# A fused scan-and-mixture kernel: identity products ahead of the first pair, the first pair's gates in halves, and another hand-set order of the first three pairs

## The chip, the cores and the metric

The kernel runs on one core of one Trainium2 chip. The metric is the device time of one execution in microseconds; the runs of the kernel before took 177.32, 178.34 and 179.44 us (median 178.34). The engines are called as in the profile: PE is TensorE, ACT is ScalarE, DVE is VectorE, POOL is GpSimd, SP issues the transfers.

## The reference, cut to what matters

Four sequences with eight heads of 768 positions and 48 channels go through a gated linear recurrence, and its output, as 3072 rows of 384 channels, through a soft mixture of 8 experts.

```python
f = 1.0 / (1.0 + np.exp(-f_logit))
for t in range(S):
    state = f[:, :, t, :, None] * state + np.einsum('bhd,bhe->bhde', k[:, :, t], v[:, :, t])
    y[:, :, t] = np.einsum('bhd,bhde->bhe', q[:, :, t], state)
...
logits = x @ phi
d = softmax of logits over the rows;  slot_input = d.T @ x
slot_out[e] = np.maximum(slot_input[e] @ w1[e], 0.0) @ w2[e]
c = softmax of logits over the slots; return c @ slot_out
```

## The kernel before, in words

The 32 heads are handled as 16 pairs, two heads side by side in the partitions (112 rows used), 768 positions along the free dimension in six chunks of 128. A pair has these steps, each with a short name in the planner:

- loads of f, k, q and v (`lf`, `lk`, `lq`, `lv`), each one transfer on SP's queue.
- The gates. `e` and `ln` (lines 312, 315, ACT): exp and logarithm, with the sum of the exp kept as a guard. `L` (line 319, DVE): the running sum of the logarithms inside each chunk, restarted by a tile `starts` of ones and zeros. `g` and `p` (lines 322, 325, ACT): its exp with both signs, into `gb` and `pb`. `dk` and `dq` (lines 329, 333, POOL): k and q times those. `pbx` and `pend` (lines 342, 339, POOL): the chunk-end values of `pb`, spread for the state scan, and kept as a guard.
- The products. `kt` (line 347, PE): six transposes of k, copied to `kta` by `kte` (line 305, DVE). `sc` (line 359, PE) in two halves of three chunks: the scores, masked by `mask` (line 364, DVE). `kv` (line 393, PE): each chunk's contribution to the state; `scan` (line 397, DVE) runs the state over the chunks. `ia` (line 384, PE) and `ie` (line 407, PE): y from the masked scores and from the state of the chunk before. `ye` (line 305, ACT) copies y out.
- For the mixture: `lg` (line 439) the logits, `xtr` and `xe` (lines 418, 305) the transposed rows. After each four pairs a batch's softmax and slot sums follow. The expert products (`up`, `down`) and the output come behind the last pair.

The pairs overlap: while PE is in pair i, the gates of pairs i+1 to i+3 are under way. Buffers rotate (three of `fb`, `kb`, `qb`; two of `Lb`, `gb`, `pb`, `pbx`). PE's results go to five units of PSUM, which a product takes and the last reader frees.

The order of each engine's queue is set by a planner, run when the program is built: every step of the pairs has one engine and a due time (`z = 7 i` us plus an offset), and on each engine the fixed steps are emitted in order of due time. Weight loads and the end are placed by the planner's estimates of durations, as are the moments to which weight loads are held back. So a changed due time moves a step in its engine's queue, and all engines work their queues in order.

Of the kernel before, what the change touches and what calls it, by code (L numbers as in the profile page):

```python
# [10 lines left out]
AF = mybir.ActivationFunctionType  # L11
ALU = mybir.AluOpType
# [4 lines left out]
NM = S // C  # L17
# [6 lines left out]
PW = 112  # L24
# [178 lines left out]
NW1 = 7  # L203


@with_exitstack
def gla_soft_moe_kernel(ctx: ExitStack, tc: tile.TileContext, q, k, f, v, vt, phi, w1, w2, out):
# [28 lines left out]
    esum = P([PW, NP], "esum")  # L236
# [66 lines left out]

    def copy(o, dst, src):
        {"ACT": nc.scalar.copy, "DVE": nc.vector.tensor_copy, "POOL": nc.gpsimd.tensor_copy}[o.eng](dst, src)  # L305
# [5 lines left out]
    def decay_exp(o, i):  # L311
        nc.scalar.activation(fb[i % N_F][:PW], fb[i % N_F][:PW], AF.Exp, scale=-1.0, accum_out=esum[:, i : i + 1])  # L312

    def decay_ln(o, i):
        nc.scalar.activation(fb[i % N_F][:PW], fb[i % N_F][:PW], AF.Ln, bias=one[:PW])  # L315

    def decay_sum(o, i):

        nc.vector.tensor_tensor_scan(Lb[i % N_L][:PW], flat(starts)[:PW], fb[i % N_F][:PW], 0.0, op0=ALU.mult, op1=ALU.add)  # L319

    def decay_g(o, i):
        nc.scalar.activation(gb[i % N_G][:PW], Lb[i % N_L][:PW], AF.Exp)  # L322

    def decay_p(o, i):
        nc.scalar.activation(pb[i % N_P][:PW], Lb[i % N_L][:PW], AF.Exp, scale=-1.0)  # L325

    def decay_k(o, i):
        t = kb[i % N_K][:PW]
        nc.gpsimd.tensor_tensor(t, t, gb[i % N_G][:PW], op=ALU.mult)  # L329

    def decay_q(o, i):
        t = qb[i % N_Q][:PW]
        nc.gpsimd.tensor_tensor(t, t, pb[i % N_P][:PW], op=ALU.mult)  # L333
# [7 lines left out]
    def decay_pbx(o, i):  # L341
        nc.gpsimd.tensor_copy(pbx[i % N_S][:PW, :, : NM - 1], ends(i)[:, : NM - 1].unsqueeze(1).broadcast_to([PW, D, NM - 1]))

    def kt(o, i):
        u = unit(("kt", i))
        for m in range(NM):
            nc.tensor.transpose(u[:, C * m : C * m + PW], kb[i % N_K][:PW, C * m : C * m + C], ident[:PW, :PW])  # L347
# [353 lines left out]

    op("consts", {"DVE": 0.5}, lambda o: consts(), w=["same"], due=30)
    op("consts_2", {"POOL": 1.0}, lambda o: consts_2(), w=["emask"], due=40)

    def attention(i):

        z = i * T
        F_, L_, G, PB = ("fb", i % N_F), ("Lb", i % N_L), ("gb", i % N_G), ("pb", i % N_P)
        K, Q, V, Y = ("kb", i % N_K), ("qb", i % N_Q), ("vb", i % N_V), ("yT", i % N_Y)
# [47 lines left out]
    def mixture(b, z):  # L757
# [97 lines left out]
    PENDS = [(n, i) for i in range(NP) for n in ("pends", "esum")]  # L855
# [38 lines left out]
    order = plan.run(dict(POOL=2.0, DVE=1.0, ACT=1.3))  # L894
# [20 lines left out]
    by_pair = [[o for o in order if first_op[i] <= o.n < first_op[i] + 28 and o.name in ("ye", "lg", "xtr", "xe")] for i in range(NP)]  # L915
# [115 lines left out]
```

## Time and profile before

| what | value |
|---|---|
| runs | 177.32, 178.34, 179.44 us |
| profiled execution | 179.07 us, span 177.3 us |
| PE busy | 153.5 us, 87% |
| DVE busy | 111.8 us, 63% |
| ACT busy | 94.6 us, 53% |
| POOL busy | 94.0 us, 53% |
| from HBM, to HBM | 48.87 MB, 4.72 MB, 302 GB/s over the span |
| pair 0, first transpose to pair 1's first | 11.52 to 21.04 us |
| steady pair | 6.30 us |

The page has one line for each engine with its busy share in forty slices of 4.43 us. The chain of work that ended last is followed back from the end: each row has its start, its length, and the engine, tile and line. The timeline has start, length, engine, line, operation and output<-inputs, and in brackets how long the engine was idle before and what ended that. The table of windows has, for each stretch, its length, the busy time of an engine with its count of instructions, the granted clock of PE as a share (PEclk), the share of the transfer engines and GB/s. The granted clock is read as 1.00 before its first record in this execution, so the start's clock is read from the durations of PE's instructions instead.

### The profile page before, as it was taken

What the parts mean: (1) busy time and instruction counts of PE and PEld (TensorE: products, weight loads), DVE (VectorE), ACT (ScalarE), POOL (GpSimd) and SP (SyncE); (2) the same over time, 40 slices, a digit from 0 to 9 for tenths busy, and PEclk for the clock granted to TensorE, in tenths of its full rate; (3) what the DMA queues carried; (4) which work ended last, traced back from release to release, by engine and by line L of the source; (5) the groups of instructions that cost most, each with busy time, mean ns of one, the idle gap of its engine ahead of it and who ended that gap; (6) DMA issues with size and microseconds to landing.
All of it is one profiled execution on the core that took longest, in us unless ns stands there. A gap on an engine that the chain in (4) does not pass through costs nothing.

```text
span 177.3 us, 6018 instructions
## 1 busy us (share of the span) xinstructions
PE 153.5 (87%) x2538; PEld 123.0 (69%) x2538; DVE 111.8 (63%) x161; ACT 94.6 (53%) x164; POOL 94.0 (53%) x91
## 2 busy tenths in 40 slices
PE   0039999999899999999999999999899999987830
PEld 0029899889689887898896988787645448555720
DVE  2569697797996795989986977956320420552320
ACT  3995279668579576794976784132521210261510
POOL 3099999998759959786898895801000000100000
PEclk9999999999999999999999999999999999999875
DMA  5999999999999999999986569999993870058580
GB/s 180 352 409 358 332 330 322 408 398 401 387 403 384 384 379 398 374 398 398 325 274 189 180 203 352 385 354 380 398 401 133 269 263 4 4 229 311 214 324 12
DMA packets 20324, 54.08 MB, mean 305 GB/s; under 512 B 2256, under 2 KB 2368, under 8 KB 20288
## 3 DMA queue, kind: packets, MB, share of 16 engines
q1 hardware_dynamic: 20288, 53.60, 82.2%
q8 instruction: 22, 0.36, 0.8%
q14 instruction: 14, 0.11, 0.2%
HBM read 48.87 MB, written 4.72 MB: 302 GB/s over the span
## 4 chain that ended last, share of the span: by engine, by line
PE 77%; DVE 6%; issue 4%; POOL 4%; ACT 4%; DMA 2%; POOLq 0%; DVEq 0%; ACTq 0%
PE sc L359 13%; PE y L384 13%; PE y L407 7%; PE kv L393 6%; PE po L644 6%; PE up L600 6%; PE kt L347 5%; PE pf L688 5%; PE xt L418 4%; PE pl L439 3%; POOL ce L525 2%; DMA fb<-in_f_dram 2%; PE pi L482 2%; DVE same L294 1%; PE turn L617 1%
## 5 line engine op out<-in xcount | busy, mean ns | idle before, releaser
L329 POOL TENSOR_TENSOR kb<-kb,gb 112x768 f32<-112x768 f32 x16 | 41.3, 2582 | 13.7 <-ACT gb L322 12.8
L319 DVE TENSOR_TENSOR_SCAN Lb<-starts,fb 112x768 f32<-112x768 f32 x16 | 30.0, 1873 | 6.2 <-ACT fb L315 6.1
L333 POOL TENSOR_TENSOR qb<-qb,pb 112x768 f32<-112x768 f32 x16 | 30.1, 1881 | 4.5 <-ACT pb L325 4.5
L364 DVE TENSOR_TENSOR scb<-sc,mask 128x768 f32<-128x768 f32 x32 | 29.1, 951 | 4.1 <-PE sc L359 4.0
L359 PE MATMUL sc<-qb,kb 48*128 48x128 f32 x384 | 27.6, 291 | 1.6 <-DVE kta L305 1.2
L384 PE MATMUL y<-scb,va 128*64 128x128 f32 (+1 forms) x384 | 27.1, 285 | 0.4 <-DVE scb L364 0.4
L305 ACT COPY yT<-y 112x768 f32<-112x768 f32 x16 | 12.8, 800 | 27.3 <-PE y L407 27.3
L525 POOL TENSOR_TENSOR ce<-ce,cm 128x256 f32<-128x256 f32 x4 | 5.1, 1272 | 41.8 <-DVE cm L522 41.2
L359 PEld LDWEIGHTS sc<-qb,kb 48*128 48x128 f32 x384 | 24.0, 196 | 4.4 <-DVE kta L305 1.5
L384 PEld LDWEIGHTS y<-scb,va 128*64 128x64 f32 (+1 forms) x384 | 23.3, 135 | 1.0 <-issue 0.5
L347 PE MATMUL kt<-ident,kb 112*128 112x112 f32 x96 | 13.0, 274 | 11.5 <-POOL kb L329 11.5
L305 DVE COPY kta<-kt 128x672 f32<-128x672 f32 x16 | 13.7, 854 | 13.3 <-PE kt L347 13.3
L347 PEld LDWEIGHTS kt<-ident,kb 112*128 112x128 f32 x96 | 10.1, 145 | 12.5 <-POOL kb L329 11.5
L315 ACT ACTIVATE fb<-fb,one 112x768 f32<-112x768 f32 x16 | 15.0, 937 | 0.6
L393 PE MATMUL kv<-va,kta 128*64 128x48 f32 (+1 forms) x384 | 15.0, 225 | 0.0
L312 ACT ACTIVATE fb<-fb 112x768 f32<-112x768 f32 x16 | 13.4, 840 | 2.8 <-DMA fb<-in_f_dram 2.8
L407 PE MATMUL y<-qb,sb 48*48 48x128 f32 x320 | 14.6, 285 | 0.0
L393 PEld LDWEIGHTS kv<-va,kta 128*64 128x64 f32 (+1 forms) x384 | 13.0, 135 | 2.0 <-issue 0.2
L325 ACT ACTIVATE pb<-Lb 112x768 f32<-112x768 f32 x16 | 13.5, 845 | 0.0
L322 ACT ACTIVATE gb<-Lb 112x768 f32<-112x768 f32 x16 | 13.2, 828 | 0.0
L407 PEld LDWEIGHTS y<-qb,sb 48*48 48x48 f32 x320 | 11.1, 162 | 2.9 <-DVE sb L397 2.2
L305 ACT COPY xb<-xt 128x576 f32<-128x576 f32 x16 | 10.2, 639 | 5.0 <-PE xt L418 5.0
(145 smaller groups left out, 253.9 us busy)
## 6 DMA issues: line engine op xcount, KB each, us to landing
w1b<-in_w_dram SPq DMA_DIRECT2D x34, 384.0 KB, 6.8
fb<-in_f_dram SPq DMA_DIRECT2D x16, 384.0 KB, 6.2
kb<-in_k_dram SPq DMA_DIRECT2D x16, 384.0 KB, 6.5
qb<-in_q_dram SPq DMA_DIRECT2D x16, 384.0 KB, 6.5
va<-in_v_dram SPq DMA_DIRECT2D x16, 288.0 KB, 6.7
out_dram<-w1b SPq DMA_DIRECT2D x12, 384.0 KB, 3.0
scb<-in_w_dram SPq DMA_DIRECT2D x4, 384.0 KB, 5.8
fb<-in_w_dram SPq DMA_DIRECT2D x3, 384.0 KB, 3.8
```

Source lines behind the costliest of these rows:

```text
L305: {"ACT": nc.scalar.copy, "DVE": nc.vector.tensor_copy, "POOL": nc.gpsimd.tensor_copy}[o.eng](dst, src)
L315: nc.scalar.activation(fb[i % N_F][:PW], fb[i % N_F][:PW], AF.Ln, bias=one[:PW])
L319: nc.vector.tensor_tensor_scan(Lb[i % N_L][:PW], flat(starts)[:PW], fb[i % N_F][:PW], 0.0, op0=ALU.mult, op1=ALU.add)
L325: nc.scalar.activation(pb[i % N_P][:PW], Lb[i % N_L][:PW], AF.Exp, scale=-1.0)
L329: nc.gpsimd.tensor_tensor(t, t, gb[i % N_G][:PW], op=ALU.mult)
L333: nc.gpsimd.tensor_tensor(t, t, pb[i % N_P][:PW], op=ALU.mult)
L347: nc.tensor.transpose(u[:, C * m : C * m + PW], kb[i % N_K][:PW, C * m : C * m + C], ident[:PW, :PW])
L359: nc.tensor.matmul(u[:, 512 * r + C * m : 512 * r + C * m + C], kb[i % N_K][rs, cs], qb[i % N_Q][rs, cs], start=True, stop=True,)
L364: nc.vector.tensor_tensor(scb[i % N_SC][:, :, h], un["sc", i, h].rearrange("p (r x) -> p r x", r=2)[:, :, : 3 * C].rearrange("p r (m t) -> ...
L384: nc.tensor.matmul(u[rows(at), y_cols(m)], va[:, v0 : v0 + (D if at else 64)], scb[i % N_SC][:, r, h, m % 3], start=m % 3 == 0, stop=False ...
L393: nc.tensor.matmul(u[rows(r), :, m], ktb[i % N_KT][:, m, rows(r)], vb[i % N_V][:, m, r], start=True, stop=True)
L407: nc.tensor.matmul(u[at : at + D, y_cols(m)], sb[i % N_S][rs, :, m - 1], qb[i % N_Q][rs, C * m : C * m + C], start=False, stop=m in (2, 5) ...
```

## The change

Three things, all at the start of the program:

1. A new step `warm` ahead of everything on PE: four products of the identity with itself, repeated to 512 columns, into a PSUM unit that nobody reads.
2. Pair 0's f is loaded in two halves of 384 positions, and its gates run in halves: `e`, `ln`, `L`, `g`, `p`, `dk`, `dq` twice. POOL keeps only the second half's `dk`; the first half's `dk`, both halves of `dq` and `pbx` go to DVE. The transposes of pair 0 run as two halves of three chunks, and its first scores need only the first half's k and q. The guard sum gets a seventeenth column.
3. The due times of pairs 0, 1 and 2 are set by a table, `START`. In all later pairs `L` is due 7 us later and `g` 2 us later, `p` 0.6 us later (`pie`, a copy in the mixture, 1.2 us earlier).

```diff
+N_WARM = 4
...
+    def warm_up(o):
+
+        u = unit(("warm",))
+        for n in range(N_WARM):
+            nc.tensor.matmul(u[:, :512], ident, ident.unsqueeze(1).broadcast_to([128, 4, 128]), start=True, stop=True)
...
-    def decay_ln(o, i):
-        nc.scalar.activation(fb[i % N_F][:PW], fb[i % N_F][:PW], AF.Ln, bias=one[:PW])
+    def decay_ln(o, i, cs):
+        t = fb[i % N_F][:PW, cs]
+        nc.scalar.activation(t, t, AF.Ln, bias=one[:PW])
...
+    def times(o, t, by):
+        (nc.vector if o.eng == "DVE" else nc.gpsimd).tensor_tensor(t, t, by, op=ALU.mult)
+
+    def decay_k(o, i, cs):
+        times(o, kb[i % N_K][:PW, cs], gb[i % N_G][:PW, cs])
...
-        nc.gpsimd.tensor_copy(pbx[i % N_S][:PW, :, : NM - 1], ends(i)[:, : NM - 1].unsqueeze(1).broadcast_to([PW, D, NM - 1]))
+        copy(o, pbx[i % N_S][:PW, :, : NM - 1], ends(i)[:, : NM - 1].unsqueeze(1).broadcast_to([PW, D, NM - 1]))
...
+    HALVES = (slice(0, S // 2), slice(S // 2, S))
+
+    START = dict(
+        e=(-60, -59), ln=(-58, -57), g=(-55, -52), p=(-54, -51),
+        L=(-60, -59), dk=(-58, -60), dq=(-57, -55.8), mask=(-54, -53),
+        kt=(-9, -7), sc=(-8, -6),
+    )
+    START["e", 1], START["ln", 1], START["e", 2], START["g", 1], START["p", 1], START["ln", 2] = -56, -53, -50, -49, -48, -47
+    START["L", 1], START["kte", 0], START["scan", 0], START["L", 2] = -56, -55, -52, -51
+    START["ye", 0], START["g", 2], START["p", 2] = -46, -45, -44
+    START["pbx", 0], START["dk", 1], START["dq", 1], START["pend", 0] = -55.5, -56, -55, -54
...
-        op("L", {"DVE": 1.8}, decay_sum, i, r=[F_], w=[L_], due=z - 2 * T - 4.8)
-        op("g", {"ACT": 0.84}, decay_g, i, r=[L_], w=[G], due=z - 2 * T + 2.4)
...
+        usual = dict(e=-2 * T - 6.9, ln=-2 * T - 5.9, L=-2 * T + 2.2, g=-2 * T + 4.4, dk=-2 * T + 3.8, p=-2 * T + 4.8, dq=-2 * T + 5.6)
+        if i == 0:
+            for h, cs in enumerate(HALVES):
+                gates(cs, [h], {name: START[name][h] for name in usual}, NP if h else 0, (0 if h else 2, 2))
+        else:
+            gates(slice(0, S), [0, 1], {name: START.get((name, i), z + t) for name, t in usual.items()}, i, (0, 1))
+        op("pbx", {"POOL": 0.65} if i else {"DVE": 0.4}, decay_pbx, i, r=PB, w=[PX], due=START.get(("pbx", i), z - T + 0.7))
+        op("pend", {"POOL": 0.2}, decay_pend, i, r=PB, w=[("pends", i)], due=START.get(("pend", i), z - T + 1.3))
+        if i == 0:
+            for h in range(2):
+                op(("kt", "square"), {"PE": 0.33}, kt, i, 3 * h, 3 * h + 3, r=K[h : h + 1], x=[KT], w=[KK], due=START["kt"][h], take=[] if h else [(KK, "a")], ni=6)
...
-    order = plan.run(dict(POOL=2.0, DVE=1.0, ACT=1.3))
+    order = plan.run(dict(PE=2.3, POOL=2.3, DVE=2.0, ACT=2.1, SP=0.4))
```

What moves on the engines. First DVE's queue from the first scan of pair 0 to the scan behind its state, before (buffers `Lb_65`, `fb_62`, `kb_73`, `qb_76` and `pbx_83` are pair 0's):

```order
L319 SCALAR_TENSOR_TENSOR Lb_65<-starts,fb_62 112x768
L319 SCALAR_TENSOR_TENSOR Lb_66<-starts,fb_63 112x768
L319 SCALAR_TENSOR_TENSOR Lb_65<-starts,fb_64 112x768
L305 COPY kta<-kt 128x672
L364 TENSOR_TENSOR scb_80<-sc,mask 128x2x384 x2
L397 SCALAR_TENSOR_TENSOR sb_85<-kv,pbx_83 112x288
L319 SCALAR_TENSOR_TENSOR Lb_66<-starts,fb_62 112x768
```

The same stretch after:

```order
L329 SCALAR_TENSOR_TENSOR Lb_65<-starts,fb_62 112x384 x2
L338 TENSOR_TENSOR kb_73<-kb_73,gb_69 112x384
L338 TENSOR_TENSOR qb_76<-qb_76,pb_71 112x384
L329 SCALAR_TENSOR_TENSOR Lb_66<-starts,fb_63 112x768
L338 TENSOR_TENSOR qb_76<-qb_76,pb_71 112x384
L312 COPY pbx_83<-pb_71 112x48x5
L312 COPY kta<-kt 128x672
L375 TENSOR_TENSOR scb_80<-sc,mask 128x2x384 x2
L408 SCALAR_TENSOR_TENSOR sb_85<-kv,pbx_83 112x288
L329 SCALAR_TENSOR_TENSOR Lb_65<-starts,fb_64 112x768
```

Three products and the copy to `pbx` have come in ahead of the copy of the transposes, and the scan of pair 2 (`fb_64`) has gone from ahead of that copy to behind the state scan of pair 0; the later scans follow one pair later in the same way. On POOL, from its first product to pair 2's first, before:

```order
L329 TENSOR_TENSOR kb_73<-kb_73,gb_69 112x768
L333 TENSOR_TENSOR qb_76<-qb_76,pb_71 112x768
L342 COPY pbx_83<-pb_71 112x48x5
L339 COPY pends<-pb_71 112x6
L329 TENSOR_TENSOR kb_74<-kb_74,gb_70 112x768
L333 TENSOR_TENSOR qb_77<-qb_77,pb_72 112x768
```

and after:

```order
L338 TENSOR_TENSOR kb_73<-kb_73,gb_69 112x384
L338 TENSOR_TENSOR kb_74<-kb_74,gb_70 112x768
L338 TENSOR_TENSOR qb_77<-qb_77,pb_72 112x768
L350 COPY pends<-pb_71 112x6
L312 COPY pbx_84<-pb_72 112x48x5
L350 COPY pends<-pb_72 112x6
```

Of pair 0 (`kb_73`, `qb_76`) POOL has one half product left, and pair 1's two products stand right behind it. On ACT, from pair 0's exp to pair 2's logarithm, after:

```order
L321 ACTIVATE fb_62,esum<-fb_62 112x384 x2
L325 ACTIVATE fb_62<-fb_62,one 112x384 x2
L321 ACTIVATE fb_63,esum<-fb_63 112x768
L332 ACTIVATE gb_69<-Lb_65 112x384
L335 ACTIVATE pb_71<-Lb_65 112x384
L325 ACTIVATE fb_63<-fb_63,one 112x768
L332 ACTIVATE gb_69<-Lb_65 112x384
L335 ACTIVATE pb_71<-Lb_65 112x384
L321 ACTIVATE fb_64,esum<-fb_64 112x768
L332 ACTIVATE gb_70<-Lb_66 112x768
L335 ACTIVATE pb_72<-Lb_66 112x768
L325 ACTIVATE fb_64<-fb_64,one 112x768
```

Between the two halves of pair 0's `gb` and `pb` stands pair 1's logarithm (`fb_63`), which before ran ahead of both.

More of the change, by code (lines that the diff above doesn't have):

```diff
@@ L341, in decay_pbx, with kt @@
     def decay_pbx(o, i):
[L342 to L346, printed above, removed]
+        copy(o, pbx[i % N_S][:PW, :, : NM - 1], ends(i)[:, : NM - 1].unsqueeze(1).broadcast_to([PW, D, NM - 1]))
+    def kt(o, i, m0=0, m1=NM):
+        u = unit(("kt", i)) if m0 == 0 else un["kt", i]
+        for m in range(m0, m1):
             nc.tensor.transpose(u[:, C * m : C * m + PW], kb[i % N_K][:PW, C * m : C * m + C], ident[:PW, :PW])
@@ L727, in attention @@
-        op("pend", {"POOL": 0.2}, decay_pend, i, r=[PB], w=[("pends", i)], due=z - T + 1.3)
-        op(("kt", "square"), {"PE": 0.65}, kt, i, r=[K], x=[KT], w=[KK], due=z - T + 3.9, take=[(KK, "a")], ni=12)
-        op("kte", {"DVE": 0.86}, kt_copy, i, r=[KK], w=[KT], due=z - T + 4.6, free=[KK])
+        if i == 0:
+            for h, cs in enumerate(HALVES):
+                op("lf", {"SP": 0.45}, load_half, fb[0], f[0], cs, w=F_[h : h + 1], due=-99, kb=192)
+        else:
+            op("lf", {"SP": 0.45}, load, fb[i % N_F], f[i], w=F_, due=z - 25, kb=384)
@@ new lines, in attention, with gates @@
+        op("lk", {"SP": 0.45}, load, kb[i % N_K], k[i], w=K, due=z - 14, kb=384)
+        op("lq", {"SP": 0.45}, load, qb[i % N_Q], q[i], w=Q, due=z - 12, kb=384)
+        op("lv", {"SP": 0.45}, load, flat(vb[i % N_V]), v[i], w=[V], due=z - 6, kb=288)
+        def gates(cs, hs, due, n, es):
+            x = len(hs) / 2
+            F_h, L_h, G_h, PB_h, K_h, Q_h = ([t[h] for h in hs] for t in (F_, L_, G, PB, K, Q))
+            act, dve = 0.2 + 0.72 * x, 0.06 + 1.72 * x
+            by = {"POOL": 0.1 + 2.4 * x}, {"POOL": 0.1 + 1.74 * x}, {"DVE": 0.06 + 0.82 * x}
+            op("e", {"ACT": act}, decay_exp, i, cs, n, r=F_h, w=[*F_h, ("esum", n)], due=due["e"])
+            op("ln", {"ACT": act}, decay_ln, i, cs, r=F_h, w=F_h, due=due["ln"])
+            op("L", {"DVE": dve}, decay_sum, i, cs, r=F_h, w=L_h, due=due["L"])
+            op("g", {"ACT": act}, decay_g, i, cs, r=L_h, w=G_h, due=due["g"])
+            op("dk", by[es[0]], decay_k, i, cs, r=[*G_h, *K_h], w=K_h, due=due["dk"])
+            op("p", {"ACT": act}, decay_p, i, cs, r=L_h, w=PB_h, due=due["p"])
+            op("dq", by[es[1]], decay_q, i, cs, r=[*PB_h, *Q_h], w=Q_h, due=due["dq"])
@@ L730, in attention @@
         for h, key in enumerate((S0, S1)):
-            op(("sc", "rows"), {"PE": 0.7}, score, i, h, r=[K, Q], x=[SC[h]], w=[key], due=z - T + 5.3 + 0.7 * h, take=[(key, "a")], ni=24)
-            op("mask", {"DVE": 0.95}, score_mask, i, h, r=[key], w=[SC[h]], due=z - T + 6.1 + h, free=[key])
+            op(("sc", "rows"), {"PE": 0.7}, score, i, h, r=[K[h], Q[h]], x=[SC[h]], w=[key], due=START["sc"][h] if i == 0 else z - T + 5.3 + 0.7 * h, take=[(key, "a")], ni=24)
+            op("mask", {"DVE": 0.95}, score_mask, i, h, r=[key], w=[SC[h]], due=START["mask"][h] if i == 0 else z - T + 6.1 + h, free=[key])
@@ L914, in gla_soft_moe_kernel @@
     resident = [o for o in order if o.name == "lw1" and o.n < tail_from]
-    by_pair = [[o for o in order if first_op[i] <= o.n < first_op[i] + 28 and o.name in ("ye", "lg", "xtr", "xe")] for i in range(NP)]
+    by_pair = [[o for o in order if first_op[i] <= o.n < past_op[i] and o.name in ("ye", "lg", "xtr", "xe")] for i in range(NP)]
     by_batch = [[o for o in order if batch_from[b] <= o.n < (first_op[PPB * b + PPB] if b < L else 0)] for b in range(L)]
```

69 lines of the change are left out of this document (35 added, 34 removed).

## The prediction

> **What bounds the kernel now.** First the page: which engine is full, and where it is not.
>
> ```profile
> span 177.3 us, 6018 instructions
> PE 153.5 (87%) x2538; PEld 123.0 (69%) x2538; DVE 111.8 (63%) x161; ACT 94.6 (53%) x164; POOL 94.0 (53%) x91
> PE   0039999999899999999999999999899999987830
> ```
>
> TensorE (PE) is empty in the first two and a half of forty slices (11.5 us) and nearly full until the last ones. So a pair of heads costs what PE costs, and a gain can come from the head of the program or from PE's speed there. The profiled execution took 179.07 us, its span 177.3; the runs shown are 177.32, 178.34 and 179.44, so it stands 0.73 above their median. Next the chain that ended last, for the head:
>
> ```profile
> 0.79 3.50 DMA fb<-in_f_dram
> 4.32 0.94 ACT fb L312 x2
> 5.35 0.94 ACT fb L315
> 6.32 1.77 DVE Lb L319
> 8.11 0.85 ACT gb L322
> ...
> 11.42 1.84 POOL qb L333
> 13.30 2.93 PE sc L359 x24
> ...
> 17.68 2.59 PE y L384 x23
> 20.27 0.84 PE y L407 x20
> 21.11 0.72 PE kt L347 x6
> 21.83 1.54 PE sc L359 x24
> 23.37 0.77 PE kv L393 x21
> 24.14 1.38 PE y L384 x23
> 25.52 0.84 PE y L407 x20
> ...
> 33.14 0.72 PE kt L347 x6
> ...
> 39.44 0.72 PE kt L347 x6
> ```
>
> Pair 0 goes load, exp, ln, scan, exp, product, products, scores. From 13.30 on PE alone carries the chain. The 24 score products take 2.93 us in pair 0 and 1.54 in pair 1, the y products 2.59 and 1.38: PE runs at half clock until about 20.2 (the last products of pair 0 already take 0.84, as in pair 1). Then a pair takes 6.30 us (33.14 to 39.44). Hence I follow one time, the start of pair 1's kt products, 21.11 here: what it gains, the end gains, as long as the steady pairs stay bound by PE.
>
> **The change part by part.** *Halves.* SP issues are 0.46 us apart (first fence below), so half the load of f may land about 0.5 us earlier (3.8; bounds 3.5 and 4.3) and the other half at about 4.4. A half of a ScalarE step: its copies of 768 and 576 elements take 800 and 639 ns, 0.84 ns an element with some 0.16 fixed, so exp 0.52 plus its 0.19 of accumulator read, ln 0.62, exp to gb or pb 0.52. A half scan is half of 1.77, 0.89; a half product on VectorE half of the mask product's 0.95, 0.48.
>
> ```profile
> 1.60 0.29 POOL masks.py:199 TENSOR_SCALAR_AFFINE_SELECT ident<-ident 128x128 f32<-128x128 f32 x1
> ...
> 1.71 0.42 SPq L309 DMA_DIRECT2D kb<-in_k_dram  x1
> 2.17 0.43 SPq L309 DMA_DIRECT2D qb<-in_q_dram  x1
> 5.06 0.19 ACT L312 ACTIVATION_READ_ACCUMULATOR fb<-fb 112x1 f32 x1
> ...
> 11.51 3.36 DVE L319 TENSOR_TENSOR_SCAN Lb<-starts,fb 112x768 f32<-112x768 f32 x1 [1.65 <-ACT fb L315]
> 13.19 2.08 POOL L342 COPY pbx<-pb 112x240 f32<-112x240 f32 x1
> 14.79 0.83 DVE L305 COPY kta<-kt 128x672 f32<-128x672 f32 x1
> ...
> 17.80 0.76 DVE L397 TENSOR_TENSOR_SCAN sb<-kv,pbx 112x288 f32<-112x288 f32 x1 [0.46 <-PE kv L393]
> ```
> ```profile
> L364 DVE TENSOR_TENSOR scb<-sc,mask 128x768 f32<-128x768 f32 x32 | 29.1, 951 | 4.1 <-PE sc L359 4.0
> L305 ACT COPY yT<-y 112x768 f32<-112x768 f32 x16 | 12.8, 800 | 27.3 <-PE y L407 27.3
> L305 ACT COPY xb<-xt 128x576 f32<-128x576 f32 x16 | 10.2, 639 | 5.0 <-PE xt L418 5.0
> ```
>
> In the new order that gives: exp 3.8 and 4.5, ln 5.2 and 5.7, half scans 5.8 to 6.7 and to 7.6, pair 1's exp 6.3, gb and pb of the first half to 8.2, its k and q products on VectorE to 8.9. So the first half's scores start 4.4 us before the 13.30 of now. The second half does not follow: its exp to gb stands behind pair 1's ln (to 9.1) and ends at 9.5, its k product on GpSimd then meets pair 1's scan on VectorE (9.1 to 10.9).
>
> These two engines lock each other out: the scan of 11.51 took 3.36 instead of 1.77 because the q product ran until 13.25, and the pbx copy took 2.08 because it then had to wait for the scan. Whichever has waited goes next. So the second half's k product ends at 11.8 (half of 1.8 after 10.9), its q product on VectorE at 12.3, and pair 1's k product, ready since 11.8, goes ahead of pair 0's pbx copy: 12.3 to 14.1. Behind that copy VectorE's queue holds the kt copy (0.83, to 15.25), two masks (0.95 each, to 17.1) and the state scan (0.76, to 17.85). PE follows them: kv at 15.3, last y products at 17.9, and with PE at full clock pair 1's kt at 18.7.
>
> *Products of the identity.* Four times 512 columns from about 2.0 on (the identity is written at 1.89). The up products stream two such half matrices of 1,536 columns in two passes each in 5.42 us, 0.88 ns a column and pass; four times 512 in two passes is 3.6 us, and up to twice that at half clock, so they end between 5.7 and 9.3. They delay only the first half's transposes (8.4), with nothing behind: the second half's come at 11.8. They cost nothing, and they bring the clock up, if it lasts.
>
> ```profile
> 131.75 5.42 PE up L600 x64
> ```
>
> *Does it last?* After them PE has 0.3 and 0.8 us of pair 0's first half, then idles from about 9.7 to 11.8, works 1.1 us, idles from 13.1 to 15.3: some 3 of 6 us busy or less. The granted clock in four stretches of PE's windows:
>
> ```profile
> 44.05:50.88 6.83, 5.67 (x105) 1.00 1.03 393
> 160.11:166.93 6.82, 5.42 (x90) 1.00 0.59 230
> ...
> 163.52:166.93 3.41, 2.60 (x32) 1.00 0.29 110
> 166.93:170.35 3.42, 2.98 (x18) 0.50 0.98 379
> ```
>
> At 166.93 the clock falls to half behind a stretch in which PE was busy for 5.42 of 6.82 us and never idle for long; at 50.88, behind 5.67 of 6.83, it did not. The gap of the change is far emptier than either. I take it that the clock falls. The Trainium skill (TensorE: Matmul & The Clock Gate, Part 1) has the clock fall only after an idle window of about 3.4 us; by that it would last here, the gaps being near 2 us. The fall at 166.93 speaks against it; what it would give is the first rival.
>
> Fallen, it has to come back once more. Now PE works without a break from 13.30 and is at full clock at 20.2, 6.9 us later; the fastest run is 1.75 below the profiled one, as if it came 3.5 us earlier. With the change unbroken work starts at 15.3, so it comes between 18.7 and 22.1. Cold, kv to kt (3.4 us at full clock from 15.3) takes up to 6.0, so pair 1's kt starts between 18.7 and 21.3. Since such a stretch may also end as late as 16 to 17 and leave a part of that fast, I take 20.1. In a median run of now it starts at 21.11 less 0.73, 20.4. Gain: 0.3 us.
>
> *Later pairs.* From pair 3 on L is scanned a pair later and its two exps stand behind y's copy. The loop is then scan 1.73, exp 0.85, two GpSimd products of 1.84 (the k product alone taken as long as the q product), with 0.1 of hand-overs: 6.36 a pair against PE's 6.30, and the q product is done some 2.5 us before its scores need it (now some 4), a reserve that 0.06 a pair doesn't use up. One stall goes along: PE waits 1.16 us at 49.07 for the kt copy behind VectorE's consts and scan. In the new phase the scan comes up to 0.7 earlier or not at all: bounds 0 and 0.7, taken 0.3.
>
> ```profile
> 31.45 1.73 DVE L319 TENSOR_TENSOR_SCAN Lb<-starts,fb 112x768 f32<-112x768 f32 x1
> ...
> 49.07 0.94 PE L359 MATMUL sc<-qb,kb 48*128 48x128 f32 x12 [1.16 <-DVE kta L305]
> ```
>
> One more DMA issue (0.46 us on SP) pushes k and q of pair 0 back; now they land 5.1 and 5.7 us after the issues of 1.71 and 2.17, then at about 7.3 and 8.3; they are needed at 7.9 and 8.4, so it is just hidden.
>
> ```profile
> kb<-in_k_dram SPq DMA_DIRECT2D x1, 384.0 KB, 5.1
> ```
> ```profile
> qb<-in_q_dram SPq DMA_DIRECT2D x1, 384.0 KB, 5.7
> ```
>
> The tail keeps its order; only homes of late weights change, and PE did not wait for those.
>
> Sum: 178.34 - 0.3 - 0.3 = **177.8 us**; on the profiled execution's terms, between 176.3 (clock lasts: 179.07 - 2.4 - 0.4) and 179.3 (kt at 21.3, nothing won later).
>
> **The rivals.** *The clock lasts* through the gap: kt at 18.7, 1.7 before the median's 20.4, with 0.3 later: 176.3. For it: no gap is longer than about 2.2 us, and 5.67 of 6.83 was enough at 50.88. Against it: the fall at 166.93. Chance 0.25.
>
> *VectorE's pbx copy slips in before pair 1's k product.* The two are ready within half a microsecond of each other (12.3 and 11.8). Then kt copy, masks and scan come 1.8 us earlier, PE works on without a break from about 13.5, and even with a fallen clock kt starts 1.3 to 1.5 earlier than in the forecast: 176.4. Against it: in every collision above the one who waited went first. Chance 0.15.
>
> *The clock comes back a stretch late* (the other side). The scores ran unbroken from 13.30 without bringing it up at 16.75, so a first stretch of 3.4 us can fail. If, in the change, the first stretch after 15.3 fails because it holds masks' gaps, the clock returns at 22 to 25 and half of 3.4 us is lost: 177.8 + 1.7 = 179.5, slower than now. It decides as soon as the return is later than about 21.5. Chance 0.12.
>
> **How the numbers follow.** The forecast has 0.48, the rivals 0.25, 0.15 and 0.12. About 1% is what a measurement of this kernel tells from no change (176.6 and 180.1 here). Faster by over 1%: two thirds of the clock-lasts case, half of the pbx case and a twelfth of the forecast, 0.28, and 0.03 for gains in the loop that I hold too small, 0.31. Slower: a third of the late clock, and 0.05 for a GpSimd loop above 6.5 us a pair, which would eat the reserve of 2.5 us after 13 pairs: 0.09. Same: 0.60. Range: from below the two fast cases, 175.7, to the late one, 179.8; the likeliest alone is 176.9 to 178.7.
>
> **What would show it.** In the new profile: scores of the first half before 10 us and of the second near 12.5; pair 1's scan and the second half's k product one behind the other; pbx behind pair 1's k product; y products of pair 0 at about 2.6 us for 24 (clock fallen) or 1.4 (lasted); pair 1's kt at 20.1 (18.7 or 16 to 17 in the first two rivals); then 6.3 us a pair. Wrong would be: kt of pair 1 early and the end not, which would make GpSimd's loop the bound; or the second half's gates not being late.

## The result, and the profile after

| | before | the change |
|---|---|---|
| median time | 179.00 us (20 runs, 177.32 to 179.44) | 176.82 us (20 runs, 175.38 to 177.72) |
| ratio | 1 | 0.9886, 95% interval 0.9859 to 0.9913 |
| profiled execution, its span | 179.07, 177.3 us | 176.33, 174.4 us |
| pair 1's first kt product | 21.04 us | 18.64 us |
| pair 2's kt to pair 15's kt | 26.77 to 117.03: 90.26 us | 24.36 to 114.23: 89.87 us |
| pair 15's kt to the end | 60.29 us | 60.17 us |

The change is 1.1% faster. (The ratios here and below set the runs beside those of the kernel before on the same chip, so they differ a little from quotients of medians; the median of before was 178.16 to 179.00 from one set to the next.) One run of the change with old later dues (187.87 us) was in a slower state and is left out below. The page of the changed kernel, its first lines, its busy rows in forty slices and the granted clock in tenths:

```profile
span 174.4 us, 6037 instructions
PE 156.1 (90%) x2546; PEld 122.4 (70%) x2546; DVE 118.3 (68%) x166; ACT 93.9 (54%) x169; POOL 90.5 (52%) x89
PE   5957999999899998999998999999899999987810
PEclk9996999999999999999999999999999999999995
```

PE now has work in the first three slices, and the fourth digit of the clock, 6, is a fall to half inside the start. The start row by row (start, length, engine, line, operation, output<-inputs, count, and in brackets the engine's idle time before it and what ended that):

```profile
3.30 0.52 ACT L321 ACTIVATE fb<-fb 112x384 f32<-112x384 f32 x1 [1.23 <-DMA fb<-in_f_dram]
...
8.18 0.56 DVE L338 TENSOR_TENSOR qb<-qb,pb 112x384 f32<-112x384 f32 x1 [0.34 <-DMA qb<-in_q_dram]
8.66 1.75 DVE L329 TENSOR_TENSOR_SCAN Lb<-starts,fb 112x768 f32<-112x768 f32 x1
8.79 0.94 PE L370 MATMUL sc<-qb,kb 48*128 48x128 f32 x12 [0.38 <-DVE qb L338]
9.05 2.15 POOL L338 TENSOR_TENSOR kb<-kb,gb 112x384 f32<-112x384 f32 x1 [6.81 <-ACT gb L332]
11.25 0.51 PE L358 MATMUL kt<-ident,kb 112*128 112x112 f32 x3 [1.52 <-POOL kb L338]
11.36 1.93 POOL L338 TENSOR_TENSOR kb<-kb,gb 112x768 f32<-112x768 f32 x1 [0.17 <-ACT gb L332]
11.54 1.99 DVE L312 COPY pbx<-pb 112x240 f32<-112x240 f32 x1
13.45 0.84 DVE L312 COPY kta<-kt 128x672 f32<-128x672 f32 x1
14.22 1.81 DVE L375 TENSOR_TENSOR scb<-sc,mask 128x768 f32<-128x768 f32 x2
14.35 1.30 PE L404 MATMUL kv<-va,kta 128*64 128x48 f32 x22 [1.65 <-DVE kta L312]
15.64 2.22 PE L395 MATMUL y<-scb,va 128*48 128x128 f32 x23
17.79 0.91 PE L418 MATMUL y<-qb,sb 48*48 48x128 f32 x20
18.64 0.80 PE L358 MATMUL kt<-ident,kb 112*128 112x112 f32 x6
```

The first half's scores start at 8.79, where the whole pair's started at 13.30. Then two lock-outs eat most of that lead, as the prediction had them: the second half's k product (half a tile, 2.15 us) stands against pair 1's scan, and the pbx copy (1.99) against pair 1's k product. The copy of the transposes, the masks and the scan are behind that copy on DVE. The table of windows for PE (length, busy time with its count, granted clock, transfer share, GB/s):

```profile
6.88:13.71 6.83, 3.92 (x33) 1.00 1.03 404
13.71:17.12 3.41, 2.77 (x39) 0.50 1.04 351
17.12:23.95 6.83, 6.83 (x135) 1.00 1.02 357
```

The identity products bring the clock up at 6.88; it falls at 13.71 and is back at 17.12. So a pair 1 that starts 2.40 us earlier in these two executions, and 0.5 us behind that, make up the 2.9 us between the spans. Where these come from, and how much of the 2.40 is luck of one execution, the experiments had to say.

### The profile page after: what moved, and what is told of

The parts are those of the page before. It is cut to its first block, busy times and chain, and to the rows that moved or that the text cites. A ratio compares the mean times of both kernels' runs of the same rounds, so it can differ in the third digit from the quotient of the medians.

```text
span 174.4 us, 6037 instructions
## 1 busy us (share of the span) xinstructions
PE 156.1 (90%) x2546; PEld 122.4 (70%) x2546; DVE 118.3 (68%) x166; ACT 93.9 (54%) x169; POOL 90.5 (52%) x89
## 4 chain that ended last, share of the span: by engine, by line
PE 64%; POOL 11%; DVE 9%; issue 4%; DMA 3%; ACT 3%; SPq 1%; POOLq 0%; DVEq 0%; ACTq 0%
PE sc L370 9%; PE y L395 9%; PE po L655 6%; PE up L611 6%; PE y L418 5%; PE kv L404 5%; PE kt L358 5%; PE pf L699 4%; PE xt L429 4%; POOL kb L338 3%; DMA qb<-in_q_dram 3%; POOL qb L338 3%; PE pl L450 3%; DVE Lb L329 3%; POOL ce L536 2%
## 5 line engine op out<-in xcount | busy, mean ns | idle before, releaser
L338 POOL TENSOR_TENSOR kb<-kb,gb 112x768 f32<-112x768 f32 (+1 forms) x16 | 29.7, 1853 | 24.7 <-ACT gb L332 20.2
L329 DVE TENSOR_TENSOR_SCAN Lb<-starts,fb 112x768 f32<-112x768 f32 (+1 forms) x17 | 35.0, 2065 | 3.0 <-ACT fb L325 2.9
L338 POOL TENSOR_TENSOR qb<-qb,pb 112x768 f32<-112x768 f32 x15 | 27.5, 1836 | 0.0
L370 PE MATMUL sc<-qb,kb 48*128 48x128 f32 x384 | 26.4, 282 | 1.2 <-DVE kta L312 0.8
L370 PEld LDWEIGHTS sc<-qb,kb 48*128 48x128 f32 x384 | 23.0, 188 | 3.9 <-DVE kta L312 1.0
L312 POOL COPY pbx<-pb 112x240 f32<-112x240 f32 x15 | 23.7, 1582 | 0.0
L332 ACT ACTIVATE gb<-Lb 112x768 f32<-112x768 f32 (+1 forms) x17 | 13.7, 805 | 5.9 <-DVE Lb L329 5.9
L325 ACT ACTIVATE fb<-fb,one 112x768 f32<-112x768 f32 (+1 forms) x17 | 15.1, 895 | 0.4
L321 ACT ACTIVATE fb<-fb 112x768 f32<-112x768 f32 (+1 forms) x17 | 13.7, 803 | 1.7 <-DMA fb<-in_f_dram 1.7
L335 ACT ACTIVATE pb<-Lb 112x768 f32<-112x768 f32 (+1 forms) x17 | 13.5, 793 | 0.0
```

The costliest lines, as they stand in the source:

```text
L321: nc.scalar.activation(t, t, AF.Exp, scale=-1.0, accum_out=esum[:, n : n + 1])
L325: nc.scalar.activation(t, t, AF.Ln, bias=one[:PW])
L329: nc.vector.tensor_tensor_scan(Lb[i % N_L][:PW, cs], flat(starts)[:PW, cs], fb[i % N_F][:PW, cs], 0.0, op0=ALU.mult, op1=ALU.add)
L332: nc.scalar.activation(gb[i % N_G][:PW, cs], Lb[i % N_L][:PW, cs], AF.Exp)
L338: (nc.vector if o.eng == "DVE" else nc.gpsimd).tensor_tensor(t, t, by, op=ALU.mult)
L370: nc.tensor.matmul(u[:, 512 * r + C * m : 512 * r + C * m + C], kb[i % N_K][rs, cs], qb[i % N_Q][rs, cs], start=True, stop=True,)
```

## The experiments

"The copy" is the copy of pair 0's chunk ends to pbx; kt of pair 1 and the clock's return are from each profiled execution. A gain of the profile's span is not always one of the time: see the last section.

| kernel | median, before beside it | ratio, 95% interval | kt of pair 1 | clock up (and down, up again) |
|---|---|---|---|---|
| change without identity products | 176.63, 178.16 | 0.9893, 0.9848 to 0.9938 | 19.51 | 19.27 |
| before with them | 178.43, 178.16 | 1.0001, 0.9973 to 1.0028 | 20.03 | 8.02 (11.43, 18.26), one more fall |
| change, copy on ACT | 174.58, 178.16 | 0.9782, 0.9742 to 0.9821 | 17.30 | 6.47 (13.30, 16.71) |
| the same again | 175.15, 178.50 | 0.9796, 0.9764 to 0.9828 | 18.94 | 4.78 (11.61, 18.43) |
| that without identity products | 176.57, 179.00 | 0.9896, 0.9860 to 0.9932 | 17.96 | 15.81 |
| the same again | 176.45, 178.50 | 0.9885, 0.9853 to 0.9917 | 18.23 | 17.12 |
| change, PE's gaps filled | 176.90, 179.00 | 0.9891, 0.9859 to 0.9922 | 19.14 | 7.36, lasts |
| copy on ACT, gaps filled | 174.83, 179.00 | 0.9808, 0.9766 to 0.9850 | 16.76 | 6.78, lasts |
| copy on ACT, whole gates | 176.52, 179.00 | 0.9868, 0.9833 to 0.9902 | 18.80 | 7.07 (10.49, 17.31) |
| change, products on GpSimd | 176.95, 178.50 | 0.9898, 0.9859 to 0.9937 | 19.83 | 5.11 (11.94, 18.77) |
| change, old later dues | 185.16, 178.16 | 1.0408, 1.0352 to 1.0464 | 19.31 | 5.15 (11.98, 18.80), two more falls |
| before, new later dues | 177.01, 178.50 | 0.9892, 0.9857 to 0.9928 | 19.98 | 18.10 |

**The identity products alone and gone.** From the change one line goes, and to the kernel before the same line comes:

```diff
-    op(("warm", "square"), {"PE": 1.75 * N_WARM}, lambda o: warm_up(o), due=-50, take=[(("warm",), "a")], free=[("warm",)], ni=4 * N_WARM)
```

> The change without the four identity products. Theory A (halves and queue order make the gain; the clock falls in PE's gap whether or not it was up before): pair 1's kt products start at 18.6 to 20.0 us, the clock comes up once, between 17 and 21; time 0 to 1.2 us above the change's 176.8, so 176.8 to 178.0. Rival B (the early full clock makes most of the gain): at least 1.5 us above, 178.3 or more. In both the first half's scores take twice as long; only in B does that delay what follows.

> The kernel before with only the four identity products ahead of pair 0. Theory A: PE idles from about 8 to 11.5, so the clock falls before or during pair 0's scores and returns no earlier than 16.7; gain 0 to 0.8 us against before, so 178.2 to 179.0. Rival B: pair 0 runs at full clock (scores 1.5 us, y 1.4), pair 1's kt near 18.7, gain 2 us or more, 177.0 or less.

Both came out as Theory A had it: 0.9893 without them against 0.9886 with them, and 1.0001 where they stand alone. In the second kernel the clock they bring is gone at 11.43, before pair 0's scores. That execution shows something else as well, PE's windows near 49 us:

```profile
45.56:48.98 3.42, 2.26 (x31) 1.00 1.04 393
48.98:52.39 3.41, 3.41 (x49) 0.50 1.04 397
```

The stall that the prediction names at 49.07 (1.16 us, for the copy of the transposes) stands in the first of these windows, and the clock falls behind it, with PE busy for 2.26 of 3.42 us. That pair takes 9.35 us for it, 7.73 in the kernel before, while pair 1 starts at 20.03 instead of 21.04. So the even time need not mean that nothing was won at the start; one trace can't part the two.

**The copy on another engine.** It goes from DVE's queue to ACT's, behind the second half's p:

```diff
-    START["pbx", 0], START["dk", 1], START["dq", 1], START["pend", 0] = -55.5, -56, -55, -54
+    START["pbx", 0], START["dk", 1], START["dq", 1], START["pend", 0] = -50.5, -56, -55, -54
...
-        op("pbx", {"POOL": 0.65} if i else {"DVE": 0.4}, decay_pbx, i, r=PB, w=[PX], due=START.get(("pbx", i), z - T + 0.7))
+        op("pbx", {"POOL": 0.65} if i else {"ACT": 0.4}, decay_pbx, i, r=PB, w=[PX], due=START.get(("pbx", i), z - T + 0.7))
```

> The change with pair 0's pbx copy on ScalarE, right behind the second half's exp, instead of on VectorE. Theory A (the copy holds VectorE's queue, because GpSimd's k product of pair 1 locks it out: 1.99 us instead of some 0.3): the kt copy starts near 11.9 instead of 13.45, PE works unbroken from about 12.8, pair 1's kt starts 1.0 to 1.7 earlier, time 175.2 to 176.0. Rival C (pair 0 is bound by the half clock or by k and q of pair 1, not by that copy): kt at 18.3 or later, no difference (176.5 to 177).

> The version with pair 0's pbx copy on ScalarE once more, beside the same without the identity products. Both theories: ratio to the kernel before 0.976 to 0.983.

0.9782 and, in another set, 0.9796: a full per cent under the change, the best version of all. That is 1.9 us by the ratios, more than Theory A's 0.8 to 1.6; some 0.2 of it lies outside the span (see the last section). Its start:

```profile
8.63 1.03 POOL L338 TENSOR_TENSOR kb<-kb,gb 112x384 f32<-112x384 f32 x1 [6.39 <-ACT gb L332]
8.72 2.56 DVE L329 TENSOR_TENSOR_SCAN Lb<-starts,fb 112x768 f32<-112x768 f32 x1
...
8.93 0.62 ACT L312 COPY pbx<-pb 112x240 f32<-112x240 f32 x1
...
11.65 0.84 DVE L312 COPY kta<-kt 128x672 f32<-128x672 f32 x1
...
13.62 2.79 PE L395 MATMUL y<-scb,va 128*64 128x128 f32 x23
...
14.15 0.74 DVE L408 TENSOR_TENSOR_SCAN sb<-kv,pbx 112x288 f32<-112x288 f32 x1
...
17.30 0.79 PE L358 MATMUL kt<-ident,kb 112*128 112x112 f32 x6
```

On ACT, which shares no lock with POOL here, the copy takes 0.62 us instead of 1.99. The copy of the transposes comes 1.8 us earlier than in the change, the state scan is done at 14.89, and now PE's own y products (2.79 at half clock, to 16.41) are the last. One part of it is luck: here the second half's k product slipped in 0.09 us ahead of pair 1's scan (1.03 us), while in the profiled execution of the repeat the scan went first:

```profile
8.96 1.75 DVE L329 TENSOR_TENSOR_SCAN Lb<-starts,fb 112x768 f32<-112x768 f32 x1
...
9.37 2.12 POOL L338 TENSOR_TENSOR kb<-kb,gb 112x384 f32<-112x384 f32 x1 [7.12 <-ACT gb L332]
...
18.94 0.79 PE L358 MATMUL kt<-ident,kb 112*128 112x112 f32 x6
```

That execution is the slowest of its six (176.44, median 175.15). Its copy of the transposes starts at 12.39 and kv at 13.87, 1.06 and 0.48 earlier than in the change; but its clock fell at 11.61 and was back only at 18.43, and pair 1's kt came 0.30 later. So the runs show the gain, and one trace may not.

**That version without the identity products**, twice, since its first profile had k and q of pair 0 land late.

> The version with pair 0's pbx copy on ScalarE (174.58), without the identity products. Theory A (the identity products bring a clock that is gone again at 13.3 us, before the y products of pair 0 that could use it; the end of the span does not see them): 174.2 to 175.0, the same within 0.4; pair 1's kt at 17.3 to 17.9. Rival (with the copy gone from VectorE's queue, PE is nearer the bound at the start, so the first half's scores and transposes at half clock now count): 0.6 to 1.2 more, 175.2 to 175.8.

> The same without the identity products, once more: the first time its profile had k and q of pair 0 land a microsecond later than in the other runs, so that it could not be told what the products are worth. Theory A (with the pbx copy gone from VectorE's queue, masks and y products follow the first half's scores and transposes, which take 1.65 and 0.8 us at half clock instead of 0.94 and 0.5): 0.4 to 1.0 us slower than with them, ratio 0.980 to 0.987. Rival (the late loads made the difference): within 0.3 us of it, and k and q land as early as with them.

The first time my Theory A missed and the loss was even beyond the rival's 0.6 to 1.2 us (0.9896 against 0.9782); with loads on time it was the same again (0.9885 against 0.9796, a little beyond the 0.987 of the second Theory A). By the runs the identity products are worth about 1% here. Rows of the repeat:

```profile
8.76 1.66 PE L370 MATMUL sc<-qb,kb 48*128 48x128 f32 x12
...
11.22 0.82 PE L358 MATMUL kt<-ident,kb 112*128 112x112 f32 x3 [0.80 <-POOL kb L338]
```

Cold, the scores take 1.66 instead of 0.94 and the transposes 0.82 instead of 0.51, and nothing on DVE hides that any more. In the change the masks could not begin before 14.22 whatever PE did; so the same products can be worth nothing there and something here. This reason is argued, not shown: in the profiled executions kt of pair 1 stands at 17.30 and 18.94 with the products and at 17.96 and 18.23 without, so the clock's phase covers the difference. In medians of the span it is 0.7 us (173.45 and 174.15), inside Theory A's 0.4 to 1.0; the other 0.6 between the medians lies outside the span and I can't explain it.

**Does a lasting clock pay?** More identity products into PE's gaps: in the change two behind each half's scores; in the version with the copy on ACT two behind the second half's transposes, and five instead of four ahead.

```diff
...
+    op(("fill", "square"), {"PE": 0.6 * 2}, warm_up, ("fill", -7.5), 2, due=-7.5, take=[(("fill", -7.5), "a")], free=[("fill", -7.5)], ni=4 * 2)
+    op(("fill", "square"), {"PE": 0.6 * 2}, warm_up, ("fill", -3), 2, due=-3, take=[(("fill", -3), "a")], free=[("fill", -3)], ni=4 * 2)
```

> The change with two more groups of two identity products in PE's gaps: behind the first half's scores (9.7 us) and behind the second half's (12.7 us). Theory A (the clock falls because PE is busy for too little of a 6.8 us stretch, not because of one long gap): with some 5.9 of 6.8 us busy the clock lasts, pair 0's y products take 1.4 us for 24 instead of 2.2, the last of them wait for the masks (16.03) and the state scan (16.69), pair 1's kt starts at 17.5 to 17.8 instead of 18.64, and the time is 175.6 to 176.2, about 1 us under the change. Rival 1 (the masks and the scan on VectorE bind, the clock is of no account): clock lasts, but kt at 18.3 or later and 176.5 to 177. Rival 2 (the fall has another cause than PE's gaps): clock falls near 13.7 all the same, kt at 18.6.

> The version with the pbx copy on ScalarE, with five identity products ahead instead of four and two more behind the second half's transposes, so that PE has no gap above half a microsecond from 3 to 12 us. There the y products of pair 0 took 2.8 us at half clock, from 13.6 to 16.4, while the state scan was done at 14.89: PE was the last. Theory A: the clock lasts past 13.3, the y products take 1.4 us and end with the masks at about 15.0, pair 1's kt starts at 15.8 to 16.2 instead of 17.30, time 173.0 to 173.6. Rival (a new wait takes the place, pair 1's scores, whose k and q products end at 14.1 and 15.8 us on GpSimd): kt at 17.0, time 174.3.

The clock lasts in both (here the windows, then the rows, of the first):

```profile
7.36:14.19 6.83, 5.27 (x37) 1.00 1.03 405
14.19:21.02 6.83, 6.79 (x98) 1.00 1.04 380
```
```profile
14.23 1.98 PE L309 MATMUL fill<-ident 128*128 128x512 f32 x4 [1.56 <-DVE kta L312]
...
16.14 0.84 PE L404 MATMUL kv<-va,kta 128*64 128x48 f32 x23
...
16.88 1.49 PE L395 MATMUL y<-scb,va 128*64 128x128 f32 x23
...
19.14 0.79 PE L358 MATMUL kt<-ident,kb 112*128 112x112 f32 x6
```

So the fall does come from PE's gaps, and the y products take 1.49 us instead of 2.22. The mean granted clock says the same of the other runs of the first: 0.983 to 0.991 in all six, 0.963 to 0.982 in the change's twenty. But Theory A's kt and time were missed in both kernels, because my filling cost what it won: the second group had to wait for a unit of PSUM until the copy of the transposes freed one, and two products take 1.98 us, not the 1.2 I had put down, so kv starts at 16.14 instead of 14.35. It is 1.79 late there and kt only 0.50 late, so the clock gave 1.3 us back. In the other kernel the second half's scores came 1.0 later (12.89 against 11.87) and kt 0.54 earlier (16.76 against 17.30); its 0.9808 can't be told from 0.9782 and 0.9796. Four of its six runs, at a mean granted clock of 0.983 to 0.986, took 174.10 to 174.93 us; the two at 0.974 and 0.965 took 176.17 and 176.27, and where the clock fell in those no trace shows. Filling without such a delay was not tried.

**Halves and engines.** Whole gates for pair 0 with both products on DVE, in the version with the copy on ACT; and the change with all of pair 0's half products on POOL:

```diff
-            for h, cs in enumerate(HALVES):
-                gates(cs, [h], {name: START[name][h] for name in usual}, NP if h else 0, (0 if h else 2, 2))
+            gates(slice(0, S), [0, 1], {name: START[name][0] for name in usual}, 0, (2, 2))
...
```
```diff
-        L=(-60, -59), dk=(-58, -60), dq=(-57, -55.8), mask=(-54, -53),
+        L=(-60, -59), dk=(-58, -56.5), dq=(-57, -56.2), mask=(-54, -53),
...
-                gates(cs, [h], {name: START[name][h] for name in usual}, NP if h else 0, (0 if h else 2, 2))
+                gates(cs, [h], {name: START[name][h] for name in usual}, NP if h else 0, (0, 1))
```

> The version with the pbx copy on ScalarE, with pair 0's gates whole again (one load of f, one exp, one ln, one scan, two exps) and both its products on VectorE, in the change's order otherwise. Theory A (the halves bring the first masks and the y products forward): scores of the first half at about 11.1 instead of 8.9, kt copy near 13, state scan near 16.3 instead of 14.89, pair 1's kt at 18.0 to 18.5 instead of 17.30; time 175.3 to 175.9. Rival (the gain came from the products on VectorE and the order, the halves only lengthen the gap in PE's work): kt at 17.0 to 17.5, time 174.3 to 174.9.

> The change with all products of pair 0's halves on GpSimd, none on VectorE. Theory A (VectorE's queue sets the end of the start, GpSimd has room): the first half's scores at about 10.9 instead of 8.79, the second half's at 13 to 13.5, masks done near 16.3 instead of 16.03, pair 1's kt at 18.6 to 19.2 instead of 18.64; ratio 0.989 to 0.993. Rival (GpSimd's products are what bound the start before, in the chain the q product ended at 13.26 with the scores right behind it): they are one behind the other with the scans between them, pair 1's k and q products are late too, kt at 20 or later; ratio 0.996 to 1.001.

The halves are worth about 0.8% in that version (0.9868 against 0.9782 and 0.9796), a little more than Theory A had; of these 1.4 us some 0.5 lies outside the span. Where the products of pair 0 run makes no difference that can be measured (0.9898 against 0.9886). Theory A's ratio holds, its kt of 18.6 to 19.2 doesn't: it came at 19.83, behind a clock that was back at 18.77. The times agree though POOL does them one behind the other, with a scan between them:

```profile
7.98 1.00 POOL L338 TENSOR_TENSOR kb<-kb,gb 112x384 f32<-112x384 f32 x1 [5.74 <-DMA kb<-in_k_dram]
...
8.94 2.44 POOL L338 TENSOR_TENSOR qb<-qb,pb 112x384 f32<-112x384 f32 x1
...
11.35 1.16 POOL L338 TENSOR_TENSOR kb<-kb,gb 112x384 f32<-112x384 f32 x1
...
13.45 0.86 DVE L312 COPY kta<-kt 128x672 f32<-128x672 f32 x1 [1.82 <-PE kt L358]
```

The copy of the transposes starts at 13.45 as in the change (to the hundredth by chance): DVE has less in its queue, and waits for transposes that come later, as POOL's products do.

**The later dues taken back, and alone.** First the change with the old due times of L, g and p for the pairs that the table doesn't name; then the kernel before with nothing but the new ones from pair 3 on:

```diff
-        usual = dict(e=-2 * T - 6.9, ln=-2 * T - 5.9, L=-2 * T + 2.2, g=-2 * T + 4.4, dk=-2 * T + 3.8, p=-2 * T + 4.8, dq=-2 * T + 5.6)
+        usual = dict(e=-2 * T - 6.9, ln=-2 * T - 5.9, L=-2 * T - 4.8, g=-2 * T + 2.4, dk=-2 * T + 3.8, p=-2 * T + 4.2, dq=-2 * T + 5.6)
```
```diff
-        op("L", {"DVE": 1.8}, decay_sum, i, r=[F_], w=[L_], due=z - 2 * T - 4.8)
-        op("g", {"ACT": 0.84}, decay_g, i, r=[L_], w=[G], due=z - 2 * T + 2.4)
+        op("L", {"DVE": 1.8}, decay_sum, i, r=[F_], w=[L_], due=z - 2 * T + (2.2 if i > 2 else -4.8))
+        op("g", {"ACT": 0.84}, decay_g, i, r=[L_], w=[G], due=z - 2 * T + (4.4 if i > 2 else 2.4))
...
-        op("p", {"ACT": 0.84}, decay_p, i, r=[L_], w=[PB], due=z - 2 * T + 4.2)
+        op("p", {"ACT": 0.84}, decay_p, i, r=[L_], w=[PB], due=z - 2 * T + (4.8 if i > 2 else 4.2))
```

> The change with the old due times of L, g and p from pair 3 on. Pair 0 as in the change, kt of pair 1 at 18.6 (more or less half the clock's phase). Theory A (the later due times matter little, 0.3 to 0.5 us of gain behind pair 1): time 0 to 0.8 above the change, with one late kt copy in pair 1 or 2, because two scans now stand ahead of it: 176.8 to 177.6. Rival D (the new due times carry a large part of the gain): 178 or more.

> The kernel before with nothing but the change's due times of L, g and p for pairs 3 and on. Theory A (the steady part of the change gains by these dues, whatever the start is like: between kt of pair 2 and the end it was 0.5 us shorter): 0.3 to 0.6 under the kernel before, ratio 0.9965 to 0.9985, kt of pair 2 to kt of pair 15 in 89.8 to 90.0 us instead of 90.26, and PE's wait near 49 us shorter. Rival (the steady part gained by another phase after the start): ratio 1.000, 90.2 to 90.3 us.

Taken back, they put the time 7 us above the kernel before (1.0408) and 9 above the change. Rival D's "178 or more" is met, but neither theory had the cause or the size. It is not the steady pairs, which go on at 6.30; it is the seam between pairs set by hand and pairs set by rule:

```profile
23.53 2.72 DVE L329 TENSOR_TENSOR_SCAN Lb<-starts,fb 112x768 f32<-112x768 f32 x1 [5.29 <-ACT fb L325]
...
26.17 0.83 DVE L312 COPY kta<-kt 128x672 f32<-128x672 f32 x1
...
27.05 1.31 PE L404 MATMUL kv<-va,kta 128*64 128x48 f32 x22 [5.40 <-DVE kta L312]
```

Pair 3's scan now stands ahead of pair 1's copy of the transposes in DVE's queue, and its logarithm, which the table's order has put late on ACT, comes at 23.5. DVE waits 5.29 us, PE 5.40. Pair 1 to pair 2 takes 13.69 us instead of 5.72, part of it at half clock behind the stall (25.63 to 32.46). One later pair, in which the clock falls again at 56.35, takes 9.36 instead of 7.42.

Alone, they bring what the whole change brings, as far as these runs can tell: 0.9892, three times and more what Theory A had. In the trace pair 2 to pair 15 takes 89.19 us (25.71 to 114.90; 90.26 before, 89.87 in the change), below Theory A's 89.8. The place is the stall of the prediction, behind DVE's four constant copies. First that stretch in this kernel, then in the change:

```profile
41.36 1.84 POOL L333 TENSOR_TENSOR qb<-qb,pb 112x768 f32<-112x768 f32 x1
...
43.00 1.30 DVE L294 COPY same<-ident 32x128 f32<-32x128 f32 x4
...
44.34 1.76 DVE L319 TENSOR_TENSOR_SCAN Lb<-starts,fb 112x768 f32<-112x768 f32 x1
...
45.92 1.92 PE L359 MATMUL sc<-qb,kb 48*128 48x128 f32 x24
```
```profile
40.90 1.83 POOL L338 TENSOR_TENSOR qb<-qb,pb 112x768 f32<-112x768 f32 x1
...
41.73 2.11 DVE L295 COPY same<-ident 32x128 f32<-32x128 f32 x4
...
43.88 1.76 DVE L329 TENSOR_TENSOR_SCAN Lb<-starts,fb 112x768 f32<-112x768 f32 x1
...
46.44 0.94 PE L370 MATMUL sc<-qb,kb 48*128 48x128 f32 x12 [0.85 <-DVE kta L312]
```

With the old start the constants meet only the end of POOL's q product and take 1.30; all 24 scores run through, and the stall is gone. With the new start POOL works some 0.8 us later against the rest, the constants meet its q product in the middle and take 2.11, and 0.85 of the old 1.16 stays. It is not the luck of one execution: from kt to kt this pair takes 7.35 to 7.44 us in all ten traces with the new start and the new dues, 6.61 here and 7.73 in the kernel before. So the two parts of the change don't add: the later dues take away a stall, and the new start brings most of it back. The other 1.06 us of this trace, pair 1's kt at 19.98 instead of 21.04, is hardly the edit's: what it moves, pair 3's scan and exps, stands behind pair 0's state scan, which ends at 18.44 here and at 18.56 before. The clock came up at 18.10 instead of 20.16. Between the medians lie 1.5 us, 1.9 by the ratio; this stretch explains 1.1, and what the rest is I can't say.

## Why the prediction was right and wrong

It held the sign and the range: 177.8 forecast, 176.82 measured. The gain was far too small: 0.6 us from a base of 178.34, where the runs give 2.2 (179.00 to 176.82). That the time is only 1 us off is partly luck, since the base, from three runs, stood 0.7 below the median of twenty. The change came out a little beyond the prediction's own line of 1%, a side to which it gave 0.31.

- *Halves, lock-outs, the pbx copy.* Right in kind, step by step. The first scores were forecast at 8.9 and came at 8.79; pair 1's scan and the second half's k product lock each other out, and the pbx copy waits 1.99 us behind pair 1's k product, so the rival in which it slips in first is out. By its runs, the copy on ACT shows that this wait held the start.
- *The load of f.* Mis-sized: the first exp was forecast at 3.8 with bounds 3.5 and 4.3, and began at 3.30; in the other executions with halves it was 3.10 to 3.33. Everything behind it came earlier: second half's k product done at 11.20 instead of 11.8, kv at 14.35 instead of 15.3, masks done at 16.03 instead of 17.1. The load of q, which was to be "just hidden", held the first half's q product for 0.34 us (the row at 8.18).
- *"They cost nothing, and they bring the clock up, if it lasts"; "I take it that the clock falls".* Both right for the change, by the runs with and without the identity products and by the window that ends at 13.71. That a lasting clock gives 176.3 stays open: where it lasted, the filling cost as much.
- *"So it comes between 18.7 and 22.1", the clock's return.* This step failed. I had counted 3.4 to 6.9 us of unbroken work from kv's start, the upper figure from one execution. It came at 17.12, 2.77 us after kv's start, behind a window in which PE was busy for 2.77 of 3.41 us: neither the 3.4 nor the unbroken work was needed. It is 3.41 us after the fall; in other executions it was 3.41 or 6.83. So kt was forecast at 20.1 and came at 18.64.
- *The start, as a term: 0.3 us.* Too small in the trace, by the two steps above: 2.40 there. But part of that is the luck of two executions: kt of pair 1 stands at 21.04, 20.03 and 19.98 in three with the old start, and at 18.64, 19.31 and 19.51 in three with the new (the second with the old later dues, the third without identity products), 1.2 us apart in the mean. "A median run of now" at 20.4 came from three runs, of which the profiled execution was 0.73 above the median; over 20 runs it is 0.07 above it.
- *Later pairs: 0.3 us from one stall.* In the change's trace 1.16 became 0.85. That this fits so well is luck too: the pairs from 2 to 15 gained 0.39 in all, and among the others two took 0.4 us longer and two 0.3 and 0.7 less. What I did not see is that the dues alone would have taken all of it, and that the start's order gives it back; nor that without them the new start would lose 8 us at its seam. The loop that I feared on POOL did not come: 6.30 a pair.
- *The clock a stretch late*, the slower side: nothing of it, no later than 19.27 with the new start, except where PE stood still.

Taken together: the change's 1.1% (0.9859 to 0.9913) can't be told from what its later dues give alone (0.9857 to 0.9928). The new start, some 1.2 us better at pair 1 by those six executions, pays for the stall it brings back (0.85) and for 0.2 us outside the span; what remains of it is too small for these runs. With the pbx copy off DVE it is worth another per cent.

## What to carry to other kernels

Look for what stands in the queue behind a small copy: a copy that takes 0.6 us on ACT took two on DVE, behind a long product on POOL, and its move to an idle engine brought as much as the whole change. When a start is ordered by hand, check the seam to the pairs ordered by rule, and try each part alone: parts that move the same stall don't add. Compare the start of several executions before a difference of a microsecond there is called a gain; two profiles can differ by that with nothing changed ahead.

## What the hardware showed that I had not expected

The granted clock changes on a grid of 3.41 us, and where the grid lies differs from one execution to the next. The Trainium skill (TensorE: Matmul & The Clock Gate, Part 1) says the window runs free; this agrees: the changes lie 3.41 us or a multiple apart, and the grid lies elsewhere each time. It says too that the clock falls after an idle window, and there the runs disagree. Of the ten falls seen in the first 60 us, one stands behind a window in which PE was idle throughout (first two rows, of the change with old later dues); but it also fell behind a window with 2.26 us of work (last two rows, the same execution), as in the kernel before with identity products:

```profile
22.21:25.63 3.42, 0.00 (x0) 1.00 0.98 322
25.63:32.46 6.83, 5.41 (x68) 0.50 0.99 375
52.93:56.35 3.42, 2.26 (x35) 1.00 1.04 393
56.35:59.76 3.41, 3.41 (x48) 0.50 1.03 386
```

No share of busy time parts falls from others: in the profiled execution of before a window with the same stall, 2.26 of 3.42 us, did not bring it down. Nor does busy time alone part the returns: in the repeat of the copy on ACT PE worked for all of two windows (6.82 of 6.82 us from 11.61) before the clock was back, in the change for 2.77 us of one. That stays open.

The time outside the span differs from kernel to kernel. Time less span has a median of 1.74 to 1.76 us in the runs of the kernel before, 1.73 with the new later dues alone, 1.75 with the identity products alone, and 1.69 to 1.75 with the copy on ACT, gaps filled or not. But it is 1.97 in the change, 1.98 without its identity products, 2.10 with its gaps filled or all products on GpSimd, 2.15 with the old later dues and 2.20 with whole gates. The version on ACT without identity products has 1.97 in one set and 2.43 in the other, so the kernel alone doesn't set it. Up to 0.7 us of a difference between kernels here is in no row of a profile, and nothing that I ran says why.
